# Attention and soft MoE on one core: moving copies from ScalarE and GpSimd to VectorE, other places for the transposes, token-major logits for the last batch, and contiguous first-layer weights

## The chip, the cores and the metric

The kernel runs on one core of a Trainium2 chip. The metric is device time in microseconds (us). The engines are PE (TensorE matmul), PEld (its weight load), DVE (VectorE), ACT (ScalarE), POOL (GpSimd) and SP (SyncE). The profile also records the clock that PE was granted, as a share of full speed.

## The reference

Causal attention over 4 batches, 8 heads, 768 tokens and head size 64, in which some heads see only the first 4 tokens and a window of 64. A soft mixture of experts follows, over all 3072 tokens with 512 features, 32 slots and 8 experts.

```python
scores = scale * np.matmul(q, k.transpose(0, 1, 3, 2))
...                                   # causal, or causal and (sink or window), by head
a = np.exp(scores - max); a /= a.sum(-1) + 1e-09
x = (a @ v) as (B*S, H*D)             # 3072 x 512
logits = x @ phi                      # 3072 x 32
d = exp(logits) / sum over tokens
slot_input = (d.T @ x).reshape(E, S_per_e, D)     # 8 experts, 4 slots each
for e in range(E):
    h = np.maximum(slot_input[e] @ w1[e], 0.0)    # 512 -> 1024
    slot_out[e] = h @ w2[e]                       # 1024 -> 512
c = exp(logits) / sum over slots
return c @ slot_out                   # 3072 x 512
```

## The kernel before

Heads are worked on in pairs: 16 pairs, each in six groups g = 0 to 5 of score blocks. While pair n runs, q, k and v of pair n+1 are transposed on PE into PSUM and copied out; ACT copies k, DVE copies q and v:

```python
if w == "k":
    self.nc.scalar.copy(o, i)
else:
    self.nc.vector.tensor_copy(o, i)
```

The main loop places this work among the groups. The two PSUM buffers of the scores ("sc") and the two of the transposes ("tr") matter to the argument:

```python
for g in range(NG):
    at.qk(n, g)                                   # scores on PE, exp on ACT
    ...
    if n + 1 < NP:
        if g < 3:
            at.transpose(n + 1, "qkv"[g])
        elif g == 4:
            at.v_blocks(n + 1)
    ...                                           # logits, dispatch of the batch before: g == 3
    if g == 5 and n >= 1:
        at.x_transpose(n - 1)
    m, pg = (n, g - 2) if g >= 2 else (n - 1, g + 4)
    at.pvmm(m, pg)                                # PV, two groups behind the scores
    if pg == NG - 1:
        at.norm(m)                                # reciprocal, then xb on DVE
    if g < 3:
        at.mask(n, g)
```

After a batch's four pairs, the logits are made slot by token, exponentiated into `expB`, and put into another token order for the output by a copy on GpSimd. `expT` is written with a step of 8 elements, 16 bytes:

```python
nc.scalar.activation(eb, lg[:, :768], ACT.Exp, accum_out=self.colpart[:, b:b + 1])
nc.gpsimd.tensor_copy(self.expT[:, b, :].rearrange("c (i p s) -> c i s p", i=6, s=8),
                      eb.rearrange("c (i s p) -> c i s p", i=6, s=8))
```

The bridge turns the last batch into the experts' inputs. Layer one then reads each expert's weights with a step of 8 elements, which puts the hidden units in the order that layer two wants:

```python
w = w1s[4 * e4 + g][:, do, :].rearrange("p (fi fo) -> p fo fi", fo=8)
nc.tensor.matmul(hp[32 * g:32 * (g + 1)], siT[:, do, :], w[:, 4 * c:4 * c + 4, :],
                 start=(do == 0), stop=(do == 3))
```

The softmax here doesn't subtract the row's maximum and nothing guards it: scores larger than these inputs give would overflow.

## Time and profile before

| what | before |
|---|---|
| time, median of 4 runs | 178.57 us (177.97 to 179.31) |
| span of the profiled run | 176.7 us, mean clock 0.947 |
| busy: PE, DVE, ACT, POOL | 78%, 62%, 68%, 32% of the span |
| attention: first and last start of xb | 20.45 and 126.09 us |
| last xb to the start of layer one | 10.29 us |
| layer one | 14.80 us |
| start of layer two, start of output | 152.94, 157.51 us |
| output, to the end of the span | 19.2 us |

Busy shares are averages over three stages that have different limits, so they do not say what bounds the kernel. The page's chain of work that ended last does more: it walks back from the last instruction, at each step to what released it. Its share by engine:

```profile
PE 35%; DVE 25%; issue 13%; ACT 11%; POOL 4%; DMA 2%; POOLq 2%; DVEq 0%; ACTq 0%
```

The chain alternates between PE, DVE and ACT. "Issue" is time in which an engine waited for nothing that the profile shows. By line, layer one's matmul (L408) has 8%, as much as any line of attention.

One measure is used throughout. The start of a pair's normalisation `xb` on DVE marks the pair, and the distance between two such starts is the pair's period. Before, the fifteen periods were 6.83 to 6.86 us, with three kinds of exception: 7.94 to 7.96 for a pair with logits, 7.25 for a pair with a dispatch (the matmuls that add a batch's tokens into the slots), and 5.61 for the last.

### The profile page before, as it was taken

Reading aid. Unit: us, or ns where it says so; the run is one execution under the profiler, and the core shown is the slowest. Engines: PE = TensorE matmul, PEld = TensorE weight load, DVE = VectorE, ACT = ScalarE, POOL = GpSimd, SP = SyncE. Lnnn points to the kernel's source line nnn. Section 1 sums busy time; section 2 is a strip of 40 time slices with the busy share of each in tenths; the row PEclk is TensorE's granted clock in tenths of the full one; section 3 lists DMA queues with packets and bytes.
Section 4 is the critical chain, followed back from the end, with each engine's and each line's share of the span. In section 5 each row is a group of like instructions: output and inputs, shape, how many; then the busy total and the mean of one; then the engine's idle time right before and its main releaser. Section 6 shows DMA issues by size and latency. Waiting matters only on the chain.

```text
span 176.7 us, 5200 instructions
## 1 busy us (share of the span) xinstructions
PE 137.3 (78%) x2228; PEld 84.7 (48%) x2228; DVE 109.5 (62%) x239; ACT 119.3 (68%) x186; POOL 57.2 (32%) x89
## 2 busy tenths in 40 slices
PE   0599898898898989889889898895663999879200
PEld 0376565665665756657566565663421111443000
DVE  0989998788658697694877966758506010339500
ACT  2167899999989999999998898997420101229300
POOL 7936913241529550506941101930025000000000
PEclk9999999999999999999999999999976599999955
DMA  4993999999999999999999999489999700008995
GB/s 53 160 178 31 158 206 211 204 217 204 212 222 207 202 225 196 217 208 217 200 222 199 214 221 208 52 171 219 211 213 210 145 0 0 4 0 356 414 412 242
DMA packets 14422, 32.87 MB, mean 186 GB/s; under 512 B 1856, under 2 KB 11072, under 8 KB 12480
## 3 DMA queue, kind: packets, MB, share of 16 engines
q0 software_dynamic: 12960, 26.25, 80.9%
q1 hardware_dynamic: 1440, 6.30, 8.8%
q8 instruction: 17, 0.28, 0.6%
q14 instruction: 5, 0.04, 0.1%
HBM read 52.50 MB, written 6.29 MB: 333 GB/s over the span
## 4 chain that ended last, share of the span: by engine, by line
PE 35%; DVE 25%; issue 13%; ACT 11%; POOL 4%; DMA 2%; POOLq 2%; DVEq 0%; ACTq 0%
PE hp L408 8%; DVE xb L143 7%; PE sc L96 7%; PE pv L129 6%; ACT pT L105 6%; DVE pT L118 5%; ACT pT L101 5%; DVE ot L455 4%; PE tpb L83 3%; DVE msk L301 3%; DMA kr<-in_k_dram 2%; PE lg L161 2%; DVE vb L85 2%; POOL expT L166 2%; POOLq L488 2%
## 5 line engine op out<-in xcount | busy, mean ns | idle before, releaser
L105 ACT ACTIVATE pT<-sc,fb 128x512 bf16<-128x512 f32 (+1 forms) x96 | 50.9, 622 | 7.2 <-PE sc L96 7.0
L101 ACT ACTIVATE pT<-sc 128x1024 bf16<-128x1024 f32 (+1 forms) x48 | 46.2, 969 | 2.9 <-PE sc L96 2.2
L129 PE MATMUL pv<-vb,pT 128*128 128x65 bf16 x672 | 37.6, 196 | 10.2 <-DVE xb L143 10.0
L96 PE MATMUL sc<-qT,kT 64*128 64x256 bf16 (+3 forms) x320 | 36.4, 290 | 3.7 <-ACT pT L105 1.1
L129 PEld LDWEIGHTS <-pT 128*128 128x128 bf16 x672 | 27.8, 99 | 18.3 <-DVE xb L143 12.1
L166 POOL COPY expT<-expB 128x768 bf16<-128x768 bf16 x4 | 14.5, 3628 | 38.0 <-ACT expB L164 38.0
L118 DVE TENSOR_TENSOR pT<-pT,msk 128x1024 bf16<-128x1024 bf16 (+1 forms) x32 | 20.1, 628 | 3.1 <-ACT pT L101 2.9
L59 POOL DMA_DIRECT2D qr<-in_q_dram x16 | 10.4, 650 | 20.5 <-DMA w<-in_moe_w_dram 9.4
L75 ACT COPY kT<-tpk 128x768 bf16<-128x768 bf16 x16 | 12.7, 793 | 5.8 <-PE tpk L68 5.8
L96 PEld LDWEIGHTS <-kT 64*128 64x128 bf16 x320 | 12.2, 95 | 8.9 <-issue 1.3
L143 DVE TENSOR_TENSOR xb<-pv,rs 128x768 bf16<-128x768 f32 x16 | 15.3, 958 | 0.6
L408 PE MATMUL hp<-w,siT 128*32 128x512 bf16 x64 | 14.8, 1088 | 0.4 <-DVE siT L400 0.4
L85 DVE COPY vb<-tpb 128x768 bf16<-128x768 bf16 x16 | 8.9, 557 | 8.7 <-PE tpb L83 8.6
L77 DVE COPY qT<-tpq 128x768 bf16<-128x768 bf16 x16 | 8.9, 556 | 7.3 <-PE tpq L68 7.2
L68 PE MATMUL tpq<-ident,qr 96*64 96x96 bf16 x256 | 9.1, 218 | 4.8 <-DMA qr<-in_q_dram 4.8
L154 DVE COPY xT<-tpx 128x768 bf16<-128x768 bf16 x16 | 8.9, 558 | 6.0 <-PE tpx L152 5.9
L114 DVE TENSOR_TENSOR pT<-pT,msk 128x512 bf16<-128x512 bf16 x32 | 12.0, 417 | 0.0
L413 ACT ACTIVATE hs<-hp,emask 128x512 bf16<-128x512 f32 x2 | 1.4, 687 | 15.6 <-PE hp L408 15.6
L59 POOL DMA_DIRECT2D vr<-in_v_dram x16 | 10.1, 632 | 3.2 <-PE tpb L83 1.7
L68 PEld LDWEIGHTS <-qr 96*64 96x64 bf16 x256 | 6.9, 117 | 8.0 <-DMA qr<-in_q_dram 4.8
L59 POOL DMA_DIRECT2D kr<-in_k_dram x16 | 10.2, 634 | 1.7 <-issue 0.9
L415 DVE TENSOR_SCALAR hs<-hp,emask 128x512 bf16<-128x512 f32 x2 | 1.5, 752 | 14.1 <-PE hp L408 14.1
(76 smaller groups left out, 168.7 us busy)
## 6 DMA issues: line engine op xcount, KB each, us to landing
w<-in_moe_w_dram POOLq DMA_DIRECT2D x15, 1024.0 KB, 15.3
out_dram<-ot SPq DMA_DIRECT2D x7, 768.0 KB, 6.4
qr<-in_q_dram POOLq DMA_DIRECT2D x16, 192.0 KB, 11.0
kr<-in_k_dram POOLq DMA_DIRECT2D x16, 192.0 KB, 11.1
vr<-in_v_dram POOLq DMA_DIRECT2D x16, 192.0 KB, 11.1
w<-in_moe_w_dram POOLq DMA_DIRECT2D x2, 512.0 KB, 24.8
out_dram<-ot SPq DMA_DIRECT2D x1, 512.0 KB, 2.7
out_dram<-ot SPq DMA_DIRECT2D x1, 256.0 KB, 2.1
```

Source lines behind the costliest of these rows:

```text
L59: self.nc.gpsimd.dma_start(t[:96], self.src[w][b, h:h + 2].rearrange("h (p s) d -> p h (s d)", s=8))
L68: self.nc.tensor.transpose(tp[64 * i:64 * (i + 1), s * 96:(s + 1) * 96], src[:96, i, s * 64:(s + 1) * 64], self.ident[:96, :96])
L75: self.nc.scalar.copy(o, i)
L85: self.nc.vector.tensor_copy(self.vbufs[n % 3][:, :, :, :64], tp.rearrange("p (j h d) -> p h j d", j=6, h=2))
L96: nc.tensor.matmul(sc[:, hh, c:c + ni * P], kT[po:po + 64, j * P:(j + 1) * P], qT[po:po + 64, i0 * P:(i0 + ni) * P], start=True, stop=True)
L101: nc.scalar.activation(pT[:, :, :L], sc[:, :, :L], ACT.Exp, scale=self.scale)
L105: nc.scalar.activation(pT[:, hh, :L], sc[:, hh, :L], ACT.Exp, scale=self.scale, bias=fb[:, h + hh:h + hh + 1])
L118: nc.vector.tensor_mul(pT[:, :, :L], pT[:, :, :L], self.msk[:, h:h + 2, c:c + L])
L129: self.nc.tensor.matmul(pv[:, hh, i * 65:(i + 1) * 65], pT[:, hh, o:o + P], vb[:, hh, j, :65], start=first, stop=True, skip_group_check=True)
L143: nc.vector.tensor_mul(xo, pv[:, :, :, :64], rs.to_broadcast([P, 2, 6, 64]))
L166: nc.gpsimd.tensor_copy(self.expT[:, b, :].rearrange("c (i p s) -> c i s p", i=6, s=8), eb.rearrange("c (i s p) -> c i s p", i=6, s=8))
L408: nc.tensor.matmul(hp[32 * g:32 * (g + 1)], siT[:, do, :], w[:, 4 * c:4 * c + 4, :], start=(do == 0), stop=(do == 3))
```

## The change

Its intent, as the edits suggest: unload ACT and GpSimd in attention; fill PE's waits with transposes; shorten the bridge; and let PE read weights at full rate. The core of the diff, with cuts marked by "...":

```diff
-        if w == "k":
-            self.nc.scalar.copy(o, i)
-        else:
-            self.nc.vector.tensor_copy(o, i)
+        self.nc.vector.tensor_copy(o, i)
...
-                if n + 1 < NP:
-                    if g < 3:
-                        at.transpose(n + 1, "qkv"[g])
-                    elif g == 4:
-                        at.v_blocks(n + 1)
+                if g == 0:
+                    at.v_blocks(n)
+                if n + 1 < NP and 2 <= g <= 4:
+                    at.transpose(n + 1, "qkv"[g - 2])
...                                  # logits, dispatch: g == 3 becomes g == 1; row sums: r == 3, g == 4 becomes r == 2, g == 5
+    def exp_slots(self, b, direct):
+        ...
+        if direct:                   # last batch: ACT writes expT itself, with the 16-byte step
+            nc.scalar.activation(o, lg, ACT.Exp, accum_out=self.colpart[:, b:b + 1])
+            return
+        nc.scalar.activation(eb, lg, ACT.Exp, accum_out=self.colpart[:, b:b + 1])
+        nc.vector.tensor_copy(o, eb) # other batches: VectorE instead of GpSimd
...
+        at.token_logits(b, range(3)) # last batch: token by slot straight from PE, no transposition of exp
+        at.logits(b, range(3))
         at.x_transpose(n)
-        at.logits(B - 1)
-        at.exp_tokens(B - 1)
-        at.dispatch(B - 1)
+        at.token_logits(b, range(3, 4))
+        at.exp_token_logits(b)
+        at.logits(b, range(3, 4))
+        at.exp_slots(b, True)
+        at.dispatch(b, slot_bf)
...
-        nc.vector.tensor_scalar_mul(slot_sc, slot_acc, rcol)
+        nc.vector.tensor_scalar_mul(escale, emask, rcol)   # scaling folded into the Relu
...
-                            w = w1s[4 * e4 + g][:, do, :].rearrange("p (fi fo) -> p fo fi", fo=8)
-                            nc.tensor.matmul(hp[32 * g:32 * (g + 1)], siT[:, do, :],
-                                             w[:, 4 * c:4 * c + 4, :], ...)
+                            nc.tensor.matmul(hp[32 * g:32 * (g + 1)], siT[:, do, :],
+                                             w1s[4 * e4 + g][:, do, c * 512:(c + 1) * 512], ...)
...                                  # 16 transposes of hs become 32, read with a step of 8 elements
```

It also loads phi by SyncE and copies it by DVE, issues the last weight loads at pair 13 instead of 15, and writes slot_out in one DVE copy instead of two halves on two engines.

## The prediction

> **What bounds the kernel now.** I read the page first (busy shares, slices, chain), then the timeline of one attention pair, then the timeline of everything after attention. The kernel has three stages: sixteen head pairs of attention (about 8 to 126 us), a narrow bridge and the expert layers (126 to 157.5), and the output (157.5 to 176.7). The page:
>
> ```profile
> span 176.7 us, 5200 instructions
> ...
> PEclk9999999999999999999999999999976599999955
> DMA  4993999999999999999999999489999700008995
> GB/s 53 160 178 31 158 206 211 204 217 204 212 222 207 202 225 196 217 208 217 200 222 199 214 221 208 52 171 219 211 213 210 145 0 0 4 0 356 414 412 242
> ...
> L408 PE MATMUL hp<-w,siT 128*32 128x512 bf16 x64 | 14.8, 1088 | 0.4 <-DVE siT L400 0.4
> ```
>
> A slice is 4.4 us. The DMA engines are busy until about 140 us, with two holes (31 GB/s at 13 to 18 us, 52 GB/s at 110 to 115). Then they idle until the output, which runs at 412 to 414 GB/s: output is a DMA bound, and the change leaves its bytes alone. The granted clock falls in slices 26 to 30, that is before and at the start of the first expert layer.
>
> One steady pair of attention, in the timeline (start, duration, engine, line, operation, idle before):
>
> ```profile
> 45.35 0.39 PE L96 MATMUL sc<-qT,kT 64*128 64x256 bf16 x4 [0.19 <-ACT pT L105]
> ...
> 45.89 2.12 ACT L101 ACTIVATE pT<-sc 128x1024 bf16<-128x1024 f32 x2
> ...
> 46.98 0.69 DVE L118 TENSOR_TENSOR pT<-pT,msk 128x1024 bf16<-128x1024 bf16 x1 [0.17 <-ACT pT L101]
> ...
> 47.60 0.23 DVE L141 RECIPROCAL rs<-pv 128x12 f32<-128x12 f32 x1
> ...
> 47.87 0.96 DVE L143 TENSOR_TENSOR xb<-pv,rs 128x768 bf16<-128x768 f32 x1
> 47.90 0.79 ACT L75 COPY kT<-tpk 128x768 bf16<-128x768 bf16 x1
> ...
> 48.89 0.42 PE L129 MATMUL pv<-vb,pT 128*128 128x65 bf16 x8 [0.59 <-DVE xb L143]
> ```
>
> The period is 6.86 us (xb at 34.16, 41.02, 47.87). It has two halves. From the first scores matmul (45.35) to the first PV matmul (48.89) is a chain of exp, mask, reciprocal, normalisation, 3.54 us, in which PE waits 0.59 at the end. From there to the next scores, 42.03 to 45.35, it is PE that works, 3.32 us, of which some 0.4 is waiting for ACT to free a scores buffer. ACT is busy 6.5 of 6.86 us. So the bound is a ring through ACT, DVE and PE, with ACT nearly full; no single engine's removal of 0.7 us need shorten it.
>
> After attention:
>
> ```profile
> 126.09 0.96 DVE L143 TENSOR_TENSOR xb<-pv,rs 128x768 bf16<-128x768 f32 x1
> ...
> 130.37 0.81 ACT L164 ACTIVATE expB<-lg 128x768 bf16<-128x768 f32 x1 [4.88 <-PE lg L161]
> ...
> 131.33 3.59 POOL L166 COPY expT<-expB 128x768 bf16<-128x768 bf16 x1 [14.99 <-ACT expB L164]
> ...
> 133.62 1.58 DVE L387 TENSOR_SCALAR slot_sc<-slot_acc,rcol 128x512 bf16<-128x512 f32 x1
> 134.97 0.36 PEld L196 LDWEIGHTS <-expT 128*128 128x128 bf16 x6 [2.88 <-POOL expT L166]
> ...
> 136.38 14.80 PE L408 MATMUL hp<-w,siT 128*32 128x512 bf16 x64 [0.39 <-DVE siT L400]
> ...
> 152.94 3.64 PE L435 MATMUL sp<-w,hT 128*32 128x512 bf16 x64
> ...
> 157.51 2.59 PE L451 MATMUL op<-slot_out,expT 128*128 128x512 bf16 x10 [0.94 <-DVE slot_out L440]
> ```
>
> The reader is to see that GpSimd's copy holds the first expert layer back until 134.97, and that L408 and L435, alike in shape and count, differ by 4 times.
>
> **What the Trainium skill says.** (1) "SBUF — State Buffer", Door 1, the box on cachelines: 16-byte lines, and every access that goes to a new line is penalised. L408's weights step 8 bf16, 16 bytes. The trace agrees: its weight loads, one per four matmuls' turn, come every 0.90 us, at clock 0.50 and at 1.00 alike, so reading limits it; contiguous L435 takes 3.64/16 = 0.23 for four. (2) "TensorE: Matmul & The Clock Gate", Part 1: half or full clock, decided over free-running windows of about 3.4 us. The trace shows 0.50 at 128 to 130 and 134.5 to 141 us, 1.00 between. (3) The SBUF page, SBUF: two separate sides: VectorE operations in a 2-port mode keep GpSimd from writing DMA descriptors. Here GpSimd's issues take 0.58 to 0.65 us each throughout; I see no such blocking before. (4) "VectorE: DVE Perf Modes", What auto-detection actually checks: an SBUF-to-SBUF copy with one source can run on two ports. For the moved expT copy, 768 strided elements, that gives my estimate of 0.5 to 0.9 us, against GpSimd's 3.63.
>
> **The change part by part.**
>
> *Start.* GpSimd's wait for phi (4.4 us) goes, so pair 3's loads can issue at about 8 instead of 15.75 us and the first hole closes. But DVE is the limit from 13.6 to 28 us (head masks), and it now gets the k copies, 0.47 us start to start as its other copies. Two before the first normalisation ends the queue, three before the second, less the earlier start: first xb about +0.5 us, second +1.0 (28.3 against 27.30).
>
> *Steady pair.* ACT loses 0.68 us start to start. Chain half: with ACT free, scores to exp 0.44, exp to mask 1.05 (both as at 67.41 to 68.90 us, where ACT had idled), mask to reciprocal 0.63, reciprocal to xb 0.27, xb to PV 1.02: 3.41, so 0.13 saved. PE half: without waiting for ACT it holds 2.88 us of work; the respread moves two groups of 16 transposes in (0.46 each) and the v blocks out (0.35): 3.45. Sum 6.86, as before. DVE would hold five copies at 0.47, masks 1.7, normalisation 1.08: 5.1, not a bound. So k's removal from ACT is paid back by PE work moved into the half where PE is critical.
>
> *Batches.* Logits now lie where PE waits anyway: their pair costs about 0.75 above a plain one instead of 1.1 (84.75-76.79 = 7.96 against 6.86). Against this, the slot sum (0.65) holds a transpose buffer about 0.5, row sums 0.24, the tokens' transposes 0.1: 1.6 a batch against 1.1 + 0.4 = 1.5 now. Nothing gained. Phi and the rest: +0.3. Xb of the last pair: 126.1 + 1.0 + 0.3 = 127.3, call it T.
>
> *Bridge.* Token logits and slot logits of three blocks occupy PE until T+1.6 (18 x 0.044 + 6 logits matmuls of 1.06, from T-0.3), transposes 0.5, copy 0.56 (T+2.7), six token matmuls 0.4, exp 0.5 (T+3.6), dispatch 0.7, sum 0.7 (T+5.0), csum, rcol, escale 0.6, siT 0.3: layer one starts at T+6.0 = 133.3. Before it was 136.38-126.09 = 10.3. Saved 4.3: GpSimd's copy, the 1.58 us scaling and the second transposition are gone.
>
> *Layer one.* 64 contiguous matmuls, 3.6 us at full clock as L435, twice that at half; one window at half: (3.4/0.45 = 8 of 16 groups, 3.4 us) + 8 x 0.225 = 5.2. I take the middle, 4.6. Saved 10.2. Transposes double to 32 and read with a stride: layer one's end to layer two's start 1.8 becomes 2.7. Layer two 3.65 + 0.15; slot_out in one DVE copy 0.75 instead of 0.94.
>
> *Sum.* 133.3 + 4.6 + 2.7 + 3.8 + 0.75 = 145.2 instead of 157.5; output 19.2 as now: span 164.3. Time less span was 1.8 to 2.3 us: 166.5.
>
> **The rivals.** (a) *Weights become the bound.* Were attention to shorten much, layer two would wait for the last w2. Closing the holes saves (1-31/213) x 4.4 + (1-52/213) x 4.4 = 7.1 us, so loads end at 133, six us before layer two. Against it; if one hole stays, 137, still hidden. It would need attention 6 us faster too, and would put a floor of about 158 us. (b) *ACT really was the bound.* ACT busy 94% speaks for it; the 0.59 us wait of PE for xb speaks against. If 0.4 us fell from each of 14 periods: 161. (c) *DVE becomes the bound*, its copies arriving late for the two transpose buffers, or the chain half not shrinking: plus 0.3 a period is plus 4: 170.5. (d) *Half clock through the layers*: plus 2.5: 169. (e) Nothing gained at the end, hidden by another wait: I see none there, as no DMA and no other engine is busy at 141 to 157 us.
>
> **Range and chances.** The end (bridge 4.3, layer one 10.2, less 0.9) gives nearly all, and is certain to about 2.5 us; attention is worked out at +1.3 but uncertain by 4 either way. Together about 5: 161.5 to 171.5. For within 2% (over 175.4) attention would have to lose 10 us: 4%. Slower: 1%.
>
> **What would show it.** Right: xb's period stays 6.7 to 7.0 us with ACT below 90% busy and PE's wait for xb grown to about 0.9; last xb at 126 to 129; layer one 3.6 to 5.2 us; bridge about 6; no DMA hole; loads ended near 133; output still 19 us. Wrong: a period near 6.5 (rival b), or over 7.1 with PE waiting for DVE's copies (c); layer one over 7 us, meaning stride was not its limit; layer two waiting for weights (a).

## The result, and the profile after

| what | before | after |
|---|---|---|
| time, median of 4 | 178.57 us | 169.78 us (168.90 to 171.12) |
| span, mean clock | 176.7, 0.947 | 167.8, 0.958 |
| first and last start of xb | 20.45, 126.09 | 20.90, 129.33 |
| last xb to layer one | 10.29 | 7.35 |
| layer one | 14.80 | 5.22 |
| start of layer two, of output | 152.94, 157.51 | 144.31, 148.74 |

The ratio is 0.9512, with a 95% interval of 0.9435 to 0.9589. Ratios here are the mean time of one kernel's fast runs over that of the other's of the same rounds, so not quite the ratio of the medians quoted.

From last xb to output the kernel gained (157.51 - 126.09) - (148.74 - 129.33) = 12.0 us. Attention gave back 3.2. The output stage took the same 19.1 us. The page after, first by engine, then by slice (4.2 us each):

```profile
PE 128.9 (77%) x2257; PEld 85.5 (51%) x2262; DVE 119.0 (71%) x247; ACT 112.3 (67%) x170; POOL 44.9 (27%) x78
...
PEclk9999999699999999999999999999999978999965
...
GB/s 46 161 179 211 220 209 209 219 200 194 211 191 225 192 228 187 116 187 179 221 195 225 197 127 191 213 217 217 215 213 217 207 121 4 0 21 415 409 419 237
```

Work has gone from ACT and POOL to DVE. The first hole in the transfers is gone. The second is shallower (127 GB/s at 96 to 101 us), and a new one of 116 GB/s lies at 67 to 71 us. The last weight load, issued at 103.8 us, lands 34.1 us later, at 137.9, before layer two at 144.31. The clock has a dip that the kernel before did not have, in slice 7 counted from 0 (29.4 to 33.6 us).

A steady pair, in the timeline (start, duration, engine, line, operation, output and input, shape, count, idle before and its releaser):

```profile
70.11 0.39 PE L93 MATMUL sc<-qT,kT 64*128 64x256 bf16 x4
...
73.49 0.42 PE L126 MATMUL pv<-vb,pT 128*128 128x65 bf16 x8 [1.02 <-DVE xb L140]
...
74.33 3.15 ACT L102 ACTIVATE pT<-sc,fb 128x512 bf16<-128x512 f32 x6 [0.99 <-PE sc L93]
...
76.95 0.39 PE L93 MATMUL sc<-qT,kT 64*128 64x256 bf16 x4
```

The chain half is 73.49 - 70.11 = 3.38 us and the PE half 76.95 - 73.49 = 3.46; the sum is 6.84 against 6.86 before. ACT, freed of the k copies, now stands idle for 0.99 us in every pair. The time it was given is not used.

After attention:

```profile
129.33 0.96 DVE L140 TENSOR_TENSOR xb<-pv,rs 128x768 bf16<-128x768 f32 x1
...
132.20 3.58 ACT L167 ACTIVATE expT<-lg 128x768 bf16<-128x768 f32 x1
...
132.90 0.69 DVE L208 TENSOR_TENSOR slot_bf<-slot_acc,slp 128x512 bf16<-128x512 f32 x1 [1.44 <-PE slp L203]
...
135.82 0.16 DVE L406 TENSOR_REDUCE csum<-colpart 128x1 f32<-128x4 f32 x1 [2.23 <-ACT expT L167]
...
136.68 5.22 PE L433 MATMUL hp<-w,siT 128*32 128x512 bf16 x64 [0.40 <-DVE siT L421]
...
144.31 3.64 PE L462 MATMUL sp<-w,hT 128*32 128x512 bf16 x64
...
148.74 2.75 PE L477 MATMUL op<-slot_out,expT 128*128 128x512 bf16 x10 [0.80 <-DVE slot_out L466]
```

The slot inputs are ready at 132.90 + 0.69 = 133.59, but DVE then stands still for 2.23 us: the column sum waits for ACT's exp, and siT comes behind it in DVE's order. On PE the row sums of the last batch, which stand before layer one, wait for the same exp until 135.84. That exp, which writes expT directly with the 16-byte step, takes 3.58 us in the trace, where the exp into the contiguous expB took 0.81 before.

The third surprise is in the pairs that carry logits, where DVE makes the reordering copy (before: GpSimd, off the path):

```profile
51.59 1.90 DVE L172 COPY expT<-expB 128x768 bf16<-128x768 bf16 x1
51.61 2.01 POOL L59 DMA_DIRECT2D qr<-in_q_dram  x1 [3.64 <-PE tpq L68]
53.11 0.75 DVE L74 COPY qT<-tpq 128x768 bf16<-128x768 bf16 x1
```

The copy takes 1.90 us, and q's copy waits behind it until 53.11. GpSimd's DMA issue started beside it takes 2.01 us instead of the 0.64 of its next one.

### The profile page after: what moved, and what is told of

It reads as the page before. It is cut to its first block, busy times and chain, and to the rows that moved or that the text cites. A ratio compares the mean times of both kernels' runs of the same rounds, so it can differ in the third digit from the quotient of the medians.

```text
span 167.8 us, 5240 instructions
## 1 busy us (share of the span) xinstructions
PE 128.9 (77%) x2257; PEld 85.5 (51%) x2262; DVE 119.0 (71%) x247; ACT 112.3 (67%) x170; POOL 44.9 (27%) x78
## 3 DMA queue, kind: packets, MB, share of 16 engines
q1 hardware_dynamic: 1968, 6.37, 9.7%
## 4 chain that ended last, share of the span: by engine, by line
PE 35%; DVE 28%; ACT 17%; issue 7%; DMA 4%; POOL 3%; DVEq 0%; ACTq 0%; POOLq 0%
PE pv L126 8%; PE sc L93 8%; DVE xb L140 7%; ACT pT L98 6%; ACT pT L102 5%; DVE pT L115 5%; DMA kr<-in_k_dram 4%; ACT ot L479 3%; PE hp L433 3%; PE tpv L68 3%; PE tpk L68 3%; PE tpx L149 2%; DVE expT L172 2%; PE sp L462 2%; ACT expT L167 2%
## 5 line engine op out<-in xcount | busy, mean ns | idle before, releaser
L98 ACT ACTIVATE pT<-sc 128x1024 bf16<-128x1024 f32 (+1 forms) x48 | 44.6, 951 | 12.7 <-PE sc L93 11.8
L59 POOL DMA_DIRECT2D qr<-in_q_dram x16 | 13.1, 817 | 34.6 <-PE tpq L68 33.7
L93 PEld LDWEIGHTS <-kT 64*128 64x128 bf16 x320 | 10.8, 96 | 8.4 <-issue 2.1
L74 DVE COPY vT<-tpv 128x768 bf16<-128x768 bf16 x16 | 8.9, 556 | 3.9 <-PE tpv L68 3.8
L112 DVE TENSOR_TENSOR pT<-pT,msk 128x1024 bf16<-128x1024 bf16 x16 | 10.9, 682 | 0.4 <-ACT pT L98 0.4
L68 PE MATMUL tpv<-ident,vr 96*64 96x96 bf16 x256 | 9.5, 222 | 2.3 <-DVE qT L74 2.3
L68 PEld LDWEIGHTS <-vr 96*64 96x64 bf16 x256 | 7.5, 119 | 6.1 <-issue 5.7
L68 PE MATMUL tpk<-ident,kr 96*64 96x96 bf16 x256 | 9.1, 217 | 1.1 <-DVE slot_acc L206 0.5
L479 ACT ACTIVATE ot<-op,rrow 128x512 f32<-128x512 f32 x12 | 7.0, 706 | 4.2 <-PE op L477 4.2
L68 PEld LDWEIGHTS <-kr 96*64 96x64 bf16 x256 | 7.3, 116 | 4.8 <-issue 3.1
## 6 DMA issues: line engine op xcount, KB each, us to landing
w<-in_moe_w_dram POOLq DMA_DIRECT2D x2, 512.0 KB, 33.6
```

Source lines behind the costliest of these rows:

```text
L59: self.nc.gpsimd.dma_start(t[:96], self.src[w][b, h:h + 2].rearrange("h (p s) d -> p h (s d)", s=8))
L68: self.nc.tensor.transpose(tp[64 * i:64 * (i + 1), s * 96:(s + 1) * 96], src[:96, i, s * 64:(s + 1) * 64], self.ident[:96, :96])
L93: nc.tensor.matmul(sc[:, hh, c:c + ni * P], kT[po:po + 64, j * P:(j + 1) * P], qT[po:po + 64, i0 * P:(i0 + ni) * P], start=True, stop=True)
L98: nc.scalar.activation(pT[:, :, :L], sc[:, :, :L], ACT.Exp, scale=self.scale)
L112: nc.vector.tensor_mul(v, v, m)
L479: nc.scalar.activation(ot[:, i, :], op, ACT.Copy, scale=rrow[:, b, r + i:r + i + 1])
```

## The experiments

Eleven kernels ran, all with correct results, on three chips. Each is compared with the kernel before in the same rounds; where an experiment is set against the changed kernel, it is by medians. One run each of the fifth, seventh and ninth counts as slow and is left out of the ratios. The medians of the kernel before were 178.82 (first to fourth experiment), 178.90 (fifth to eighth) and 179.46 (ninth to eleventh). Unless said otherwise an experiment is the changed kernel with the edit shown.

### 1. Strided weights in layer one again

```diff
-                                             w1s[4 * e4 + g][:, do, c * 512:(c + 1) * 512],
+                            w = w1s[4 * e4 + g][:, do, :].rearrange("p (fi fo) -> p fo fi", fo=8)
+                                             w[:, 4 * c:4 * c + 4, :],
...                                          # and the 16 transposes of before
```

> The changed kernel with one part undone: layer one reads its weights with a step of 8 elements again (and its transposes are the 16 contiguous ones of before). Theory (nearly all the gain is the reading of the weights): layer one takes 14 to 15 us instead of 5.2, layer one to layer two 1.8 instead of 2.4, so the time goes up by about 9 us, to 178 to 179.5, and nearly all of the change's gain is gone. Rival (the gain is spread over attention, bridge and layer one): it goes up by less than 6 us.

179.04 us, ratio 1.0013 (0.9953 to 1.0072): the same as the kernel before. Layer one in the timeline:

```profile
137.53 14.71 PE L434 MATMUL hp<-w,siT 128*32 128x512 bf16 x64 [0.41 <-DVE siT L421]
```

Layer one takes 14.71 us, as before the change. Without contiguous weights, everything else in the change together gains nothing measurable. The clock dip of the third pair was longer here (9.12 us for that pair, against 8.21), which is 0.9 us of the loss.

### 2. The k copies back on ACT

```diff
-        self.nc.vector.tensor_copy(o, i)
+        if w == "k":
+            self.nc.scalar.copy(o, i)
+        else:
+            self.nc.vector.tensor_copy(o, i)
```

> The changed kernel with the k copy back on ScalarE, at its new place (after the scores of g=3). Theory of the ring: ACT is then busy 6.5 us of a period and its fourth, fifth and sixth exps come 0.68 us later, so the period goes from 6.85 to about 7.4 and the time up by 6 to 9 us. Rival (in the changed schedule ACT has slack enough, so the place of the k copy is free): period within 0.1 us of 6.85 and the time within 1.5 us of 169.8.

173.86 us, 0.9718 (0.9653 to 0.9782). Plain pairs take 7.52 us; last xb at 133.83, 4.5 later than in the changed kernel. In the timeline of such a pair, the next scores wait for ACT:

```profile
79.69 0.39 PE L96 MATMUL sc<-qT,kT 64*128 64x256 bf16 x4 [0.43 <-ACT pT L105]
```

With the transposes in their new places, ACT would be in the way if it had the k copies. The time rose by 4.1 us against the changed kernel, where 6 to 9 were expected. In part that is because pairs with dispatch and token transposes also take 7.52 or 7.53, so their extra work hides in ACT's excess.

### 3. The transposes back in their old places

```diff
-                if g == 0:
-                    at.v_blocks(n)
-                if n + 1 < NP and 2 <= g <= 4:
-                    at.transpose(n + 1, "qkv"[g - 2])
+                if n == 0 and g == 1:
+                    at.v_blocks(0)
+                if n + 1 < NP:
+                    if g < 3:
+                        at.transpose(n + 1, "qkv"[g])
+                    elif g == 4:
+                        at.v_blocks(n + 1)
```

> The changed kernel with the transposes of q, k, v at their old places (g=0, 1, 2) and the v blocks at g=4, and all copies still on VectorE. Theory of the ring: the half in which PE works falls back from 3.45 to 2.88 us, but the k copy now comes on DVE ahead of the reciprocal and lengthens the chain half from 3.41 by 0.47 to 3.9, so the period is 6.7 to 6.8 and the time 0 to 2 us below 169.8. Rival b of the prediction (ACT was the bound and its 0.68 us should come straight off): period 6.2 to 6.4 and the time 6 to 9 us lower. Rival (the respread was what kept the period from growing): period over 7.0, time over 172.

172.52 us, 0.9642 (0.9576 to 0.9708). Plain pairs take 7.29 us: the rival's number, not the theory's. The timeline of a pair:

```profile
73.07 0.55 DVE L74 COPY kT<-tpk 128x768 bf16<-128x768 bf16 x1
...
73.54 0.22 DVE L138 RECIPROCAL rs<-pv 128x12 f32<-128x12 f32 x1
...
74.81 0.42 PE L126 MATMUL pv<-vb,pT 128*128 128x65 bf16 x8 [1.02 <-DVE xb L140]
...
75.65 2.78 ACT L102 ACTIVATE pT<-sc,fb 128x512 bf16<-128x512 f32 x5 [1.42 <-PE sc L93]
...
78.12 0.39 PE L93 MATMUL sc<-qT,kT 64*128 64x256 bf16 x4 [0.19 <-ACT pT L102]
```

The chain half is 74.81 - 70.84 (scores) = 3.97 us, because k's copy now stands before the reciprocal on DVE; that was expected. The PE half was expected to shrink to 2.88 and stayed at 3.32. Its floor is not PE's work. ACT can start the exp of g = 3 only after the first PV and the scores behind it, and with two score buffers the next pair's scores wait for those exps, as the last line shows. So the two groups of 16 transposes that the prediction charged to the PE half mostly fill time in which PE would have waited anyway.

### 4. Another order in the bridge

csum, rcol and escale are issued after siT, and the row sums of the last batch after layer one:

```diff
-        csum = at.small.tile([P, 1], F32, tag="cs", name="csum")
-        nc.vector.reduce_sum(csum, colpart, axis=AX.X)
...
             nc.vector.tensor_copy(siT, sip)
+            csum = mlp.tile([P, 1], F32, tag="cs", name="csum")
+            nc.vector.reduce_sum(csum, colpart, axis=AX.X)
...                                  # rp and its reciprocal: after the Relus of layer one
```

> The changed kernel with two things out of layer one's way: the row sums of the last batch come after layer one on PE, and csum, rcol and escale after the siT copy on DVE. Theory: in the changed kernel layer one waited for the strided exp on ScalarE (3.1 us and its accumulator read) through DVE's and PE's order alone; it now starts 2.3 us earlier, about 7.35-2.3 = 5.0 us after the last normalisation starts, and as PE has then been idle for less, at full clock for at least part: total 2.3 to 4 us lower, 166 to 167.5. Rival (the escale of layer one's evacuation waits for the same exp, so the wait only moves): less than 1 us lower.

170.62 us, 0.9532 (0.9458 to 0.9606): no gain. The timeline shows that one wait was exchanged for another:

```profile
135.63 0.29 DVE L416 CAST siT<-sip 128x128 bf16<-128x128 f32 x1 [0.45 <-PE sip L415]
...
137.44 5.32 PE L428 MATMUL hp<-w,siT 128*32 128x512 bf16 x64 [1.90 <-ACT expT L167]
```

siT is ready 1.5 us before layer one starts, and layer one still waits for the exp. The bridge takes 137.44 - 130.50 = 6.94 us, 0.4 less than in the changed kernel, and a longer clock dip (9.46 us for the second pair) takes more than that back. The most likely reason is memory: the PSUM tile `hp` takes the place that the attention pools gave up, where the exp still reads `lg`. The run does not test that. It does show that reordering alone is not enough while the exp itself is long.

### 5. The last exp in two steps

ACT writes a contiguous buffer, and VectorE reorders it while PE works on layer one:

```diff
-        at.exp_slots(b, True)
+        at.exp_slots(b, False, False)          # exp into ebl, no copy yet
...
             nc.vector.tensor_copy(siT, sip)
+            nc.vector.tensor_copy(expT[:, B - 1, :].rearrange("c (i p s) -> c i s p", i=6, s=8), ebl)
...                                             # rp and its reciprocal: just before layer two
```

> The changed kernel with the last batch's exp written contiguously by ScalarE (as in the other batches) into a buffer of its own, the reordering copy to expT on VectorE after the siT copy (1.9 us, beside layer one), and the row sums after layer one's transposes. The reordered bridge before gained nothing because layer one's first accumulator still had to wait until ScalarE had read the logits out of the same part of PSUM. Theory (the strided exp of 3.1 us on ScalarE holds the bridge, whatever the order behind it): the exp takes 0.8 us, layer one starts about 5.0 to 5.3 us after the last normalisation starts instead of 7.35, so its end comes 2 us earlier: time 167 to 168.5, 166 to 167 if layer one also finds the full clock. Rival (something else would hold layer one back as long): 169.5 or more.

166.78 us, 0.9294 (0.9233 to 0.9355), about 3 us under the changed kernel. The timeline:

```profile
132.85 0.81 ACT L170 ACTIVATE ebl<-lg 128x768 bf16<-128x768 f32 x1
...
134.88 1.94 DVE L424 COPY expT<-ebl 128x768 bf16<-128x768 bf16 x1
135.01 3.64 PE L431 MATMUL hp<-w,siT 128*32 128x512 bf16 x64 [0.41 <-DVE siT L423]
```

The last xb was at 129.98, so the bridge took 5.03 us, within the expected range, and layer one ran at full clock. The run also moves the row sums, but that and more was done in the fourth experiment and gave 0.4 us. So the direct strided write was nearly the whole excess of the bridge. The early clock dip was longer here too (9.31 us for the second pair), so the last xb is 0.65 us later than in the changed kernel.

### 6. The scores of g = 3 before the first PV

```diff
+            early = not (n >= 5 and n % 4 == 1)
             for g in range(NG):
-                at.qk(n, g)
+                if not (early and g == 3):
+                    at.qk(n, g)
...
+                if early and g == 2:
+                    at.qk(n, 3)
```

> The changed kernel with the scores of g=3 issued on PE before the wait of the first PV matmul for xb, instead of after it, in all pairs but the three with logits. Theory of the ring as corrected by the run with the old places (the second half cannot fall below about 3.3 us while ScalarE starts its fourth exp only after the first PV, because two score buffers tie the next pair's scores to the end of the fifth exp): ScalarE then has no idle 1.0 us before its fourth exp, PE's half falls by 0.33 to 3.12 us, the plain period from 6.85 to 6.5, 11 to 12 such periods: time 3 to 4.5 us lower, 165 to 167. Rival (the period is a matter of PE's total work alone): under 1 us.

168.48 us, 0.9400 (0.9350 to 0.9451). Plain pairs fall from 6.84 to 6.51 us, which confirms the ring found in the third experiment. The time misses the 165 to 167 us expected, because only the four plain pairs and the last one (4.99 instead of 5.60) could use it: those with token transposes (7.18), dispatch (7.37) or logits (7.92 to 7.96) did not move at all. That makes 4 x 0.33 + 0.61 = 1.9 us; a longer clock dip (8.74 instead of 8.21) and a later first xb (0.47) take half of it back in the profiled run, where the last xb comes 0.9 us earlier. The medians differ by 1.3, and the intervals of the two ratios overlap: the shorter period is shown, a shorter time against the changed kernel is not.

### 7. The same, and k's transposes before the first PV

```diff
+                    if g == 2:
+                        at.transpose(n + 1, "q")
+                        ktp = at.transpose_pe(n + 1, "k")    # PE part here
...
+                if g == 2 and n + 1 < NP:
+                    at.evacuate(n + 1, "k", ktp)             # VectorE's copy after the normalisation
```

> The same, and the k transposes also on PE before that wait (their copy on VectorE after the third mask). Theory of the ring: the wait of PE for xb, about 0.8 us in the changed kernel, is filled, the second half falls to 2.7 us, the period to 6.1 to 6.3 us, where ScalarE's 5.9 us of exps becomes the next bound: time 5 to 8 us lower than 169.8, 162 to 165. Rival c (VectorE's copies come too late for the two transpose buffers): no better than the run with early scores alone.

173.60 us, 0.9662 (0.9580 to 0.9744): slower than the changed kernel. Plain pairs are down to 6.30 us (one of 6.45), near the 6.1 to 6.3 expected, but the pairs after logits take 7.75 to 9.25. The timeline of one:

```profile
57.97 0.25 DVE L201 COPY elg<-tpe 128x192 bf16<-128x192 bf16 x1
...
58.27 0.53 PE L71 MATMUL tpk<-ident,kr 96*64 96x96 bf16 x16 [1.53 <-DVE elg L201]
```

The k transposes need one of the two transpose buffers, and it is held by the tokens' transposes until DVE, behind its normalisation, copies them out. PE waits 1.53 us, and the scores of g = 3 behind it wait too. That is part of the loss: the pairs without a clock dip take 7.75 (token transposes) and 8.13 us (dispatch), against 7.18 and 7.37 in the sixth experiment. In three others the clock fell to 0.50 for 3.4 us, and they take 9.05 to 9.25.

### 8. Work that only keeps PE busy

```diff
+    def warm(self, k):
+        t = self.trp.tile([P, P], F32, tag="tr", name="warm")
+        for _ in range(k):
+            self.nc.tensor.matmul(t, self.ident, self.ident, start=True, stop=True)
...
+                if g == 2 and n < 3:
+                    at.warm(16)
...                                  # and 26 such matmuls in the bridge, before layer one
```

> The changed kernel with work without use on PE: 16 matmuls of 128 columns in each of the first three pairs where PE waits for the normalisation, and 26 after sip where it waits for ScalarE. Theory (the clock falls because PE idles through too much of a window): the slow pair at about 30 to 36 us (8.21 us, clock 0.50) falls to about 6.9, layer one starts at clock 1.00 and takes 3.6 to 4 us instead of 5.2: time 2 to 3 us lower, 167 to 168. Rival (the clock does not follow PE's load here, or the added work costs as much as it brings): within 1 us of 169.8.

167.75 us, 0.9358 (0.9300 to 0.9417), 2 us under the changed kernel, by doing more. The third pair takes 6.84 us instead of 8.21, and layer one 3.64 instead of 5.22; 0.9 of these 2.95 us is lost again at the start, where the first xb comes at 21.81 instead of 20.90. Two stretches of 3.4 us around the dip, as windows (start and end, length, busy us and count of instructions for PE, PEld, DVE, ACT and POOL, granted clock, DMA share, GB/s); the kernel before, then the changed kernel, then this one:

```profile
27.40:30.80 3.40, 2.70 (x54) 1.87 (x49) 3.02 (x6) 3.08 (x6) 1.27 (x3) 1.00 1.21 217
```

```profile
27.40:30.80 3.40, 2.06 (x54) 1.41 (x48) 3.37 (x8) 2.08 (x4) 0.85 (x2) 0.99 1.05 197
30.80:34.20 3.40, 3.40 (x46) 2.35 (x42) 1.87 (x6) 2.42 (x5) 1.06 (x2) 0.51 1.22 232
```

```profile
27.40:30.80 3.40, 3.06 (x60) 2.12 (x60) 3.37 (x7) 2.08 (x3) 0.64 (x1) 1.00 1.04 198
```

In the changed kernel PE is busy 2.06 us of the first stretch, and in the next one the clock is 0.51. DVE is full there (3.37 of 3.40): it has built head masks until 26.4 and now has k's copies as well, so its normalisation comes late and PE waits for it:

```profile
29.08 0.42 PE L126 MATMUL pv<-vb,pT 128*128 128x65 bf16 x8 [1.34 <-DVE xb L140]
```

With matmuls that nobody reads, PE is busy 3.06 us and the clock stays at 1.00: the dip comes from PE's low load. That the load is low because of k's copies on DVE fits the other runs. A dip in the second or third pair is in the changed kernel and in every variant with k's copies on DVE and no filler (experiments 1, 3 to 7); it is not in the kernel before, in the eleventh, or in the second, which has k's copies on ACT (its third pair takes 7.52 us; a dip comes later, in its fifth, 8.20).

### 9. What helped, together

The two-step exp, the early scores, the start's filler, and the reordering copy of the other batches in three pieces, placed at g = 3, 4 and 5:

```diff
-        nc.vector.tensor_copy(o, eb)
+        self.cp = (o, eb)
+
+    def copy_piece(self, k):
+        o, eb = self.cp
+        self.nc.vector.tensor_copy(o[:, 2 * k:2 * k + 2], eb[:, 2 * k:2 * k + 2])
...                                  # and the edits of 5, 6 and the start of 8
```

> What helped, together: the two-step exp of the last batch, the early scores, the 16 matmuls of filler in the first three pairs, and the copy of each batch's exp in three pieces of some 0.65 us at g=3, 4, 5, where VectorE has room, instead of 1.9 us at once ahead of the q copy. Theory: the slow early pair goes (1.4 us or more), plain pairs stay at 6.5, the logits pair falls from 7.9 to about 7.2 because no transposes wait for the q copy, layer one starts 5.0 us after the last normalisation starts: 161 to 163.5. If the parts hide one another: 165 or more.

160.41 us (159.96 to 162.66), 0.8939 (0.8876 to 0.9002). It beats both kernels, the changed one by 9 us, and lies 0.6 us below the expected range. Pairs with logits now take 7.13 to 7.18 us: cut in pieces, the copy no longer holds up q's copy. The end of it:

```profile
128.94 3.64 PE L447 MATMUL hp<-w,siT 128*32 128x512 bf16 x64 [0.41 <-DVE siT L439]
...
139.78 2.75 PE L496 MATMUL op<-slot_out,expT 128*128 128x512 bf16 x11 [0.80 <-DVE slot_out L485]
```

Its last weight load, issued at 100.1 us, lands 35.1 us later, at 135.2, and layer two starts at 135.35. That load brings half of the last expert's weights, which layer two reads last, so no wait is seen yet; but little is left before transfers begin to bind.

### 10. The same with the early k transposes

> The same with the k transposes early too, and 8 matmuls of 128 columns without use in each pair (not in the three with logits) before the early scores. Theory (the run with early k lost only through the clock, which fell to 0.50 after windows in which PE was busy for half the time): the clock stays 1.00 through attention, plain pairs 6.3 us or a little more for the added 0.4 us of work, none of 8 to 9 us: 160 to 163. Rival (the slow pairs have another cause than the clock): pairs of 8 to 9 us remain, over 166.

The edit is that of the ninth with the one of the seventh, and eight filler matmuls ahead of the scores of g = 3. 175.64 us, 0.9795 (0.9723 to 0.9866), unclear at the 2% line and far from the ninth. Pairs of 8.31 to 9.85 us remain. The rival holds, though not alone: k's transposes still wait 1.67 us for the copy of elg, and filler that stands behind the wait in PE's order cannot fill it. The clock did not stay at 1.00 either. The slow pairs show both costs: the one without a dip takes 8.31 us, those with 3.4 us at clock 0.50 take 9.61 to 9.85. So the wait comes first, and the half clock that comes after it adds some 1.3 us to a pair.

### 11. The kernel before with contiguous weights only

The edit is the layer-one part of the diff above, applied to the kernel before.

> The kernel before with one part of the change alone: layer one reads its weights contiguously, with the 32 transposes that go with it. Theory (this part is nearly the whole gain): layer one 3.6 to 5.5 us instead of 14.8, transposes 0.6 us longer: 8.5 to 10.5 us below the kernel before, 168.5 to 170.5, the changed kernel's time within 1.5 us. Rival (the parts need each other): less than 7 us.

171.67 us, 0.9593 (0.9519 to 0.9668): 7.8 us gained with this part alone, less than the 8.5 to 10.5 expected. Layer one takes 5.14 us, and the bridge still waits for GpSimd:

```profile
133.50 3.63 POOL L166 COPY expT<-expB 128x768 bf16<-128x768 bf16 x1 [17.05 <-ACT expB L164]
```

The periods are those of the kernel before except the last, 7.45 us instead of 5.61: the clock is at 0.50 from 121.2 us to 141.7, into layer one. That moved the last xb from 126.09 to 128.05 and accounts for the miss. Why the clock fell earlier than in the kernel before, whose attention is the same, stays open. PE's load does not tell them apart: just before the fall it was busy 1.86 of 3.40 us, and 1.88 of 3.41 in the same stretch of the kernel before (117.66 to 121.07), where the clock stayed at 1.00.

## Why the prediction was right, point by point

169.78 us lies in the range. The middle, 166.5, was 3.3 us too low. In the span the misses add up to 3.5 us (167.8 against 164.3); time less span was 1.7 us in the profiled runs, not the 2.2 that the sum added, which hid 0.5, and the median lies 0.3 above the profiled run. Three readings were a little off, without weight in the sum: the clock row falls in slices 29 to 31 counted from 0 (128 to 141 us), not 26 to 30; ACT was busy 6.37 us of the period shown, not 6.5; and GpSimd's issues took 0.53 to 0.79 us, not 0.58 to 0.65. Each miss has its step:

| step | predicted | measured | miss |
|---|---|---|---|
| first xb | 20.95 | 20.90 | 0 |
| second xb | 28.3 | 28.06 | -0.2 |
| from there to the last xb | 99.0 | 101.27 | +2.3 |
| bridge | 6.0 | 7.35 | +1.35 |
| layer one | 4.6 | 5.22 | +0.6 |
| its end to layer two | 2.7 | 2.41 | -0.3 |
| layer two and slot_out | 4.55 | 4.43 | -0.1 |
| output | 19.2 | 19.1 | -0.1 |

**Start: right.** The first transfer hole closed, and DVE's queue delayed the first two pairs about as worked out. What the step did not ask is what DVE's queue does to PE. PE's waits there dropped the clock, and the third pair took 8.21 us instead of 6.86: +1.35 us, a term that the sum lacked. The eighth experiment removes it with filler.

**Steady pair: right in its numbers, wrong in one cause.** Chain half 3.41 predicted and 3.38 measured, PE half 3.45 and 3.46, period 6.86 and 6.84. But "PE half: without waiting for ACT it holds 2.88 us of work; the respread moves two groups of 16 transposes in" is not what happened. The third experiment, which leaves the transposes where they were, has a PE half of 3.32 and a longer chain half. ACT and the two score buffers set that half, and the transposes lie mostly in its gaps, so that 3.45 met 3.46 was luck. "k's removal from ACT is paid back by PE work" must read: the ring has nearly the same length, because what ends it is when ACT gets the scores of g = 3. The sixth experiment starts those earlier, and the period falls to 6.51. Rival (b), that ACT was the bound, fell for the change as a whole: ACT got 0.99 us of idle time and no pair got shorter. It holds in a weaker form: with the new places, k's copies on ACT would cost 0.7 us a pair (second experiment).

**Batches: one term mis-sized.** The extra work of a batch above four plain pairs was 1.95 us against 1.6. Token transposes and dispatch were right, 0.34 + 0.51 against 0.84 together. The logits pair was not: 7.96 - 6.85 = 1.1 instead of 0.75. The term is the moved expT copy, "my estimate of 0.5 to 0.9 us", which takes 1.90 on DVE's path. In pieces (ninth experiment) the pair takes 7.15; without pieces but with early scores (sixth) it stays at 7.92 to 7.96. Three batches of 0.36 make 1.1 us.

**Bridge: an exp mis-sized, and a wait not seen.** The list of steps was right, and even 1 us too long: with the contiguous exp (fifth experiment) layer one starts at T + 5.03, not T + 6.0. But the list counted an exp of 0.5 on the path, that of the tokens, and left the direct exp of the slots beside it. It takes 3.58 us, and csum waits for it ahead of siT. Rival (e) said "hidden by another wait: I see none there"; this was one, on the engine that the change gave new work. It cost 7.35 - 5.03 = 2.3 us, of which the too long list hid 1 by luck.

**Layer one: right.** Stride was the limit: with it four matmuls took 0.88 to 0.93 us, at clock 0.50 and 1.00 alike (kernel before, first experiment). Without it 14.80 became 5.22, with eight groups of four matmuls at half clock, about 0.42 us each, and the rest at 0.22. That is the upper end of the stated 3.6 to 5.2, not the middle. At full clock it takes 3.64 (experiments 5, 8 and 9). It carries nearly the whole gain: without it the time is as before (first experiment), and alone it gives 7.8 us (eleventh).

**The other rivals.** (a) Weights did not bind; the last load landed at 137.9 us, 6.4 before layer two. But that is 3.6 earlier than before (141.5) and not the 7.1 predicted: two shallower holes stayed, worth an estimated (1 - 116/215) x 4.2 + (1 - 127/215) x 4.2 = 3.65 us. (c) DVE became the bound in the first pairs and, through the strided copy, in the logits pairs, not in plain ones. (d) Half clock lasted for half of layer one.

## What to carry to other kernels

Look first for operands that are read with a stride on the path that sets the end: one such read, 14.80 us against 5.22, was worth more here than all the redistribution of work among engines. When an operation is moved or fused, cost it by a row of the same access pattern, since the same 98 thousand elements took 0.81 or 3.58 us on ACT depending only on how they were written. And when an engine is unloaded and the period stays, trace the ring through buffers and engines: the place of one group of scores moved it (6.84 to 6.51 us), while taking the k copies off ACT, with the transposes moved as well, did not (6.86 to 6.84).

## What the Trainium skill lacked or had wrong

- "SBUF — State Buffer", Door 1: the box on cachelines names a penalty for each new 16-byte line and no size for PE, ACT or VectorE. For a 16-byte step the runs show 0.90 us for four matmuls of layer one at either clock, against 0.22 contiguous at full clock (14.71 against 3.64 us for all 64), and for the exp of 128x768 elements on ACT 3.58 us against 0.81 contiguous.
- "VectorE: DVE Perf Modes", What auto-detection actually checks: its conditions led to an estimate of 0.5 to 0.9 us for the strided SBUF-to-SBUF copy. It took 1.90 us (1.94 in the fifth experiment). A figure for strided writes is missing.
- "SBUF — State Buffer", SBUF: two separate sides: the box on DVE blocking DMA names an fp32 copy; a later section, Who interferes with whom, counts any copy that enters a 2-port mode. The runs fit the later one: beside the strided bf16 copy of 1.90 us both GpSimd issues that fell there took 2.01 and 1.96 us instead of 0.64. In the trace no wait is put down to it: the time is in the issue's own duration.
- "TensorE: Matmul & The Clock Gate", Part 1: half clock is said to come after an idle window of about 3.4 us, and a later section speaks of frequent short idles in one kernel without a size. Here PE was busy 2.06 of 3.4 us, no gap over 1.34 us, and the next stretch ran at 0.51; at 2.70 of 3.4 the clock stayed at 1.00. No threshold follows from these traces: in the changed kernel's output stage PE was busy 1.93 of 3.41 us (153.60 to 157.01) and the next 3.39 us still ran at 1.00. The stretches are ones chosen from the trace, not the hardware's own windows.
